# Two spectral-MLP layers: edge columns of z from small turns, and the turns of z at other places

## The chip, the cores and the metric

The kernel runs on one core of one Trainium2 chip. The metric is the time of one execution on the device in microseconds (us), lower is better. An execution that was profiled also has a span, from its first to its last instruction.

## The reference

The computation is one layer "A" and one layer "B", done twice, on 2048 rows (S) of 512 channels (D), with F = 1376. All data are float32.

```python
def _A_ref(x, dft_seq_re, dft_seq_im, dft_hid_re, dft_hid_im):
    a = jnp.einsum("bsd,ed->bse", x, dft_hid_re)
    b = jnp.einsum("bsd,ed->bse", x, dft_hid_im)
    y = jnp.einsum("ts,bse->bte", dft_seq_re, a) - jnp.einsum("ts,bse->bte", dft_seq_im, b)
    return y

def _B_ref(x, w1, w2, w3, w4):
    h = _gelu(_layernorm(x, axis=-1) @ w1)
    # four groups of 128 channels, shifted by +1, -1, +2, -2 rows (zeros at the ends)
    hs = jnp.concatenate([g0, g1, g2, g3], axis=-1) @ w2
    x1 = x + hs
    h2 = _gelu(_layernorm(x1, axis=-1) @ w3) @ w4
    return x1 + h2

x = A_x
x = x + _A_ref(_layernorm(x, axis=-1), ...)
x = x + _B_ref(_layernorm(x, axis=-1), ...)
# and both once more
```

## The kernel before

Every product is made of three matmuls of 128 x 512: a float32 operand is split into a high part (cast to fp32r) and a low part (the rest), and high x high, high x low and low x high are summed in PSUM (`mm3`, lines 261 to 263). ScalarE (ACT) makes the high parts, VectorE (DVE) the low parts. Instructions run on each engine in the order in which the program writes them; `hook` functions and the lists in `late` place side work between the steps of a loop. SyncE (SP) issues all transfers, in program order, and a transfer that must wait holds back the ones behind it.

A layer has these stages. The rows are cut into four chunks (c = 0 to 3) of 512.

- **x stage and y stage** of chunk c (`x_phase`, `y_phase`) multiply by the sequence matrix. Pieces of that matrix of 512 KB come through four raw buffers (`raw`, lines 190, 208 to 224) and are split into four ring buffers. A y stage is 192 matmuls. The product of chunk c with the hidden matrix (`hid`) is made inside the x stage of chunk c + 1; that of chunk 3 stands by itself after its y stage, as four steps of 24 matmuls. The operands `rr` of those steps are finished just before by DVE and ACT work called `re1`, `im1+`, `re0+` and so on (`run_late`).
- **z of a chunk** is its layer-normed rows, turned so that the channels lie on the partitions. A turn is made in parts: ACT normalizes a tile of 128 rows (line 309), DVE turns it in 32 x 32 blocks (`turn_one`, line 555), SP stores the four strips to DRAM (`turn_out`, line 563) and loads them back in the other order (`turn_in`, line 568), and `zt_split` (lines 573, 574) makes high and low parts, in two pieces of 128 x 1024. `zt[0]` and `zt[1]` hold two chunks in turn, each with two edge columns on either side (HALO) that belong to the neighbour chunks.
- **`shifted(c)`** multiplies z of chunk c by w1: four groups of 12 matmuls each, for channels shifted by -1, -2, +1 and +2 columns in that order. The first two groups read the left edge, the last two the right edge. Each group ends in a gelu (line 607) and a split (608, 609).
- **`mixed(c)`** multiplies by w2 (four blocks of 12 matmuls), adds the normed x and gives `x1s`. Those are normed and turned in the same way into `rt` (`rt_split`).
- **`mlp(c)`**: 13 steps t, most of 24 matmuls, on `rt`. `shifted`, `mixed` and the turns of the chunk after are called between its steps.

Before, z of chunk 0 is loaded from `x1d` in the x stage of chunk 3, normed and turned there, and loaded back in that chunk's y stage (k = 4). Chunk 1 is normed in the y stage, turned after the third `hid` step and loaded behind the weights w1. Chunk 2 is normed and turned in `shifted(0)` and loaded in `mixed(0)`; chunk 3 is turned in `mlp(0)`. The right edge of chunk c is copied from the loaded chunk c + 1:

```python
def right_halo(c):
    v = ztf[(c + 1) % 2][:, :, 1, HALO : 2 * HALO]
    hi, lo = (zt[c % 2][:, :, i, HALO + CH :] for i in range(2))
    nc.scalar.copy(hi, v)                                                  # line 594
    nc.vector.tensor_tensor(lo, v, hi.bitcast(F32), op=ALU.subtract)       # line 595
```

Of the kernel before, what the change touches and what calls it, by code (L numbers as in the profile page):

```python
# [13 lines left out]
P = 128  # L14
# [6 lines left out]
NC = S // CH  # L21
# [4 lines left out]
B = 32  # L26
# [9 lines left out]

FIRST, X6, X7 = (1, 3, 5, 8, 11, 13), 2, 4
HAT = (2, 3, 3, 4, 5, 5, 6, 6)
BACK = {1: (4,), 2: (6,), 4: (8,), 5: (10,)}
HORDER = ((1, 0), (0, 1), (1, 1), (0, 0))  # L40


# [1 line left out]
def spectral_mlp_kernel(ctx: ExitStack, tc: tile.TileContext, x, ws, hs, w1, w2, w34, out):  # L44
# [263 lines left out]
    def normed_act(o, s, mr):  # L308
        nc.scalar.activation(o, s, AF.Identity, bias=mr[2], scale=mr[1])  # L309
# [237 lines left out]
    def blocks_of(u):  # L547
        return u.rearrange("p (d a i) -> p d a i", d=KD, a=NB)

    def blocks_in(t, q):  # L550
        return t.rearrange("p d (a q j) -> p d a q j", a=NB, q=TC)[:, :, :, q]

    def turn_one(t, q, u=None):
        v = blocks_in(t, q)
        nc.vector.transpose(v, v if u is None else blocks_of(u))
# [9 lines left out]
    def turn_in(dst, col):  # L565

        z = zd[count["turn"] % 2].rearrange("(d p) t -> p d t", p=P)
        nc.sync.dma_start(dst[:, :, 1, col : col + CH], z)
# [18 lines left out]
        if c == NC - 1:  # L587
            nc.vector.memset(zt[c % 2][:, :, :, HALO + CH :].bitcast(F32), 0.0)

    def right_halo(c):  # L590

        v = ztf[(c + 1) % 2][:, :, 1, HALO : 2 * HALO]
        hi, lo = (zt[c % 2][:, :, i, HALO + CH :] for i in range(2))
        nc.scalar.copy(hi, v)
        nc.vector.tensor_tensor(lo, v, hi.bitcast(F32), op=ALU.subtract)
# [81 lines left out]
    pairs = [tmp[:, 2 * i : 2 * i + 2] for i in range(3)]  # L677
    X1 = pairs[2]
    Z = tmp[:, 0:4]
    singles = [tmp[:, 4], tmp[:, 5], spare[:, 0], spare[:, 1]] + [tmp[:, i] for i in range(4)]  # L680
    warm = const.tile([P, 1], F32, name="warm")
    nc.scalar.activation(warm, mhalf[:, 0, 0:1], AF.Gelu_apprx_tanh)

    for layer in range(LAYERS):
# [4 lines left out]
        for c in range(NC):  # L689
# [74 lines left out]
            def hook(i):  # L764
                k, odd = divmod(i, 2)
                if layer == 0 and c == 1:
                    if i == 1:
                        xp_sums(NP - 1)
                    if i == 2:
                        xp_highs(NP - 1, False)  # L770
                    if i == 3:
                        xp_lows(NP - 1, False)
                if c == 0:
                    if layer:
                        for k, first in ((6, X6), (7, X7)):
                            for step, f in zip((0, 1, 3, 4, 6), xp_stages):
                                if i == first + step:
                                    f(k)
                    return
                j = (c - 1) * TC  # L780
                if i == 4:
                    rows(X1, xin, j, 2, True)
                if i == 9:
                    rows(X1, x1d, j, 2, False)
                if i == 10:
                    rows(X1, xin, j + 2, 2, True)
                if c == NC - 1:
                    if i == 6:
                        for q in range(TC):
                            nc.sync.dma_start(blocks_in(Z, q), blocks_of(x1d[q * P : (q + 1) * P, :]))  # L790
                    if 0 <= i - 9 < 4:
                        u = blocks_in(Z, i - 9)
                        normed_act(u, u, ln2[i - 9])
                    if 0 <= i - 11 < 4:
                        turn_one(Z, i - 11)
                    if i == 15:
                        turn_out(Z)

            x_phase(c, hook)

            def hook(k):
                if k == 1 and c:
                    rows(X1, x1d, (c - 1) * TC + 2, 2, False)
                if c == NC - 1:
                    for j in BACK.get(k, ()):
                        rows(xs[j // 2], x1d if j < 12 else xin, j, 2, True)
                    if k == 4:
                        turn_in(ztf[0], HALO)
                    if k in (4, 5):
                        for j in (2 * k - 4, 2 * k - 3):  # L810
                            normed_act(blocks_in(Z, j - TC), blocks_of(xt(j)), ln2[j])

            y_phase(c, hook)

# [4 lines left out]
        for i, (ri, dp) in enumerate(HORDER):  # L819
            if i == 1:  # L820
                run_late("im1")
            if i == 3:
                state["limit"] += 2
            s = stream()
            hid(ri, dp, s, acc4, 0, i == 0, i == 3)
            j = (0, 2, 12, 14)[i]
            rows(xs[j // 2], x1d if j < 12 else xin, j, 2, True)
            if i == 0:
                run_late("re1", "im1+")
            if i == 1:  # L830
                run_late("re0+", "re0++")
            if i == 2:
                run_late("re0")
                for q in range(TC):
                    turn_one(Z, q)
                turn_out(Z)
                zt_split(0)
                edges(0)
                zs.update(norm_z(range(8, 10)))
        w1p = [stream(), stream()]  # L840
        turn_in(ztf[1], HALO)
        zs.update(norm_z(range(10, 12)))
        state["limit"] += 2
        w2p = [stream(), stream()]

        def hook(n):
            if n == 0:
                right_halo(0)
            turn_one(turn2, n, zs.pop(8 + n))
            if n == 3:  # L850
                turn_out(turn2)

        shifted(0, w1p, hook)
        mrs = []

        def hook(q, x1s):
            if q == 0:
                turn_in(ztf[0], HALO)
                zt_split(1)
                left_halo(2)  # L860
            if q % 2:
                mrs.extend(stats(x1s[q - 1 : q + 1]))
# [3 lines left out]
        def hook(n):  # L866
            if n == 0:
                finish_z3(0, x1s, mrs)
                for q in range(TC):
                    turn_one(turn2, q, x1s[q])  # L870
                turn_out(turn2)
                right_halo(1)
# [18 lines left out]
        for c in range(NC):  # L891
            for t in mlp(c):
                if t == 1 and c:
                    for j in range((c - 1) * TC, c * TC, 2):
                        rows(xs[j // 2], dst, j, 2, False)
                if c == 0:
                    if t == 0:
                        add_y(NC - 1, 1, PB, xs[7], "14")
                    if t in (3, 4):
                        run_late(str(6 + 2 * t))  # L900
                    if t in (5, 6):
                        zs.update(norm_z((2 + 2 * t, 3 + 2 * t)))
                    if t in (7, 8):
                        for q in (2 * t - 14, 2 * t - 13):
                            turn_one(turn_z, q, zs.pop(12 + q))
                    if t == 8:
                        turn_out(turn_z)
                    if t == 10:
                        turn_in(ztf[1], HALO)
                    if t == 11:  # L910
                        zt_split(0)
                        left_halo(NC - 1)
                    if t == 12:
                        zt_split(1)
                        edges(NC - 1)
                        right_halo_of(2)
                if c + 1 < NC:
                    if c > 0 and t == 0:
                        shifted(c + 1, w1p)
                    if c > 0 and t == 1:  # L920
                        x1s = mixed(c + 1, w2p)
                    n = t - 1 if c else t
                    if n == 1:
                        mrs = stats(x1s)
                    if n in (2, 3):
                        finish_z3(c + 1, x1s, mrs, (2 * n - 4, 2 * n - 3))
                    if n in (3, 4):
                        turn_z3(c + 1, x1s, (2 * n - 6, 2 * n - 5))
                    if n == 4:
                        turn_out(turn_r[(c + 1) % 2])  # L930
                    if n == 6:
                        turn_in(rtf[(c + 1) % 2], 0)
# [65 lines left out]
```

## Time and profile before

| | before |
|---|---|
| time, median of 3 runs | 1508.55 us (1508.46 to 1509.02) |
| the profiled execution | 1509.24 us, of which 1507.5 us are its span |
| mean granted TensorE clock | 0.992 |
| busy: PE, DVE, ACT, POOL | 98%, 74%, 45%, 6% of the span |
| moved by DMA | 246.5 MB, 164 GB/s over the span |

PE is TensorE, POOL is GpSimd, SPq is SyncE's queue of transfers. A profile row of a matmul shows its start, its length, and, in brackets, how long PE was idle before it and what ended that wait. Matmuls overlap: in a dense stream one starts every 0.227 us though each is shown with 0.39 us. The two layers run the same stages; the stage of chunk 3 that the change touches lies at about 303 to 476 us in the first layer and at about 1045 to 1220 us in the second.

### The profile page before, as it was taken

How to read it: one execution, taken by the hardware profiler on the slowest of the kernel's cores; microseconds unless marked ns; L12 is line 12 of the kernel's file. 1: busy time of each engine (PE TensorE's matmuls, PEld its weight loads, DVE VectorE, ACT ScalarE, POOL GpSimd, SP SyncE). 2: the span in 40 equal slices, each digit the busy share in tenths (PEclk: the TensorE clock that was granted, in tenths of full speed). 3: DMA queues.
4: the chain of work that ended last, by engine and by line, in shares of the span. 5: the costliest groups of instructions: out<-in, count | busy, mean ns of one | idle time of the engine just before them, and what ended most of it. 6: DMA issues, size and time to landing. Idle time of an engine off the chain costs nothing.

```text
span 1507.5 us, 17227 instructions
## 1 busy us (share of the span) xinstructions
PE 1471.5 (98%) x6408; PEld 1207.6 (80%) x6408; DVE 1123.0 (74%) x1548; ACT 684.8 (45%) x873; POOL 89.1 (6%) x101
## 2 busy tenths in 40 slices
PE   9999999999888999999999999999989799999998
PEld 7888888887777888887888888888867688888887
DVE  6876987979757756568899879899878576654553
ACT  5564454554444443335544544445535254332331
POOL 2100000000001100001100000000000010000000
PEclk9999999999999999999999999999999899999999
DMA  7336656587553534333435565655776437243440
GB/s 238 125 100 199 211 171 225 169 238 259 201 168 116 161 129 126 103 114 107 137 127 187 190 218 173 208 202 163 230 261 210 126 123 208 83 128 98 126 147 35
DMA packets 127156, 246.50 MB, mean 164 GB/s; under 512 B 24544, under 2 KB 57312, under 8 KB 127072
## 3 DMA queue, kind: packets, MB, share of 16 engines
q1 hardware_dynamic: 127072, 245.40, 50.7%
q8 instruction: 50, 0.82, 0.2%
q14 instruction: 34, 0.28, 0.1%
HBM read 213.91 MB, written 31.46 MB: 163 GB/s over the span
## 4 chain that ended last, share of the span: by engine, by line
PE 82%; DVE 10%; DMA 4%; issue 2%; ACT 2%; SPq 0%; POOL 0%; DVEq 0%; ACTq 0%; POOLq 0%
PE psd L263 9%; PE psd L262 9%; PE psd L261 9%; PE psa L262 8%; PE psa L261 8%; PE psa L263 8%; PE psc L261 6%; PE psb L263 6%; PE psc L262 6%; PE psc L263 6%; PE psb L262 5%; PE psb L261 5%; DVE ring L224 3%; DMA raw<-in_ws 2%; DMA zt1f<-zd 1%
## 5 line engine op out<-in xcount | busy, mean ns | idle before, releaser
L208 ACT CAST ring<-raw 128x1024 fp32r<-128x1024 f32 (+1 forms) x231 | 226.7, 987 | 184.0 <-PE psb L263 110.4
L224 DVE TENSOR_TENSOR ring<-raw,ring 128x1024 fp32r<-128x1024 f32 (+1 forms) x231 | 262.9, 1143 | 27.1 <-ACT ring L208 27.1
L608 DVE CAST h<-tmp 128x512 fp32r<-128x512 f32 x70 | 29.8, 426 | 101.8 <-ACT tmp L607 101.8
L607 ACT ACTIVATE tmp<-psd 128x512 f32<-128x512 f32 x60 | 35.8, 596 | 132.7 <-PE psd L263 90.3
L261 PE MATMUL psd<-ring,rr 128*128 128x512 f32 x208 | 80.9, 389 | 0.0
L262 PE MATMUL psd<-ring,rr 128*128 128x512 f32 x208 | 80.9, 389 | 0.0
L263 PE MATMUL psd<-ring,rr 128*128 128x512 f32 x208 | 80.9, 389 | 0.0
L263 PE MATMUL psd<-rt,ring 128*128 128x512 f32 x176 | 68.6, 390 | 0.6 <-DVE ring L224 0.6
L263 PE MATMUL psa<-rt,ring 128*128 128x512 f32 x176 | 68.6, 390 | 0.0
L261 PE MATMUL psd<-rt,ring 128*128 128x512 f32 x176 | 68.5, 389 | 0.0
L262 PE MATMUL psd<-rt,ring 128*128 128x512 f32 x176 | 68.5, 389 | 0.0
L262 PE MATMUL psa<-rt,ring 128*128 128x512 f32 x176 | 68.5, 389 | 0.0
L261 PE MATMUL psa<-rt,ring 128*128 128x512 f32 x176 | 68.5, 389 | 0.0
L261 PE MATMUL psc<-ring,h 128*128 128x512 f32 x176 | 68.5, 389 | 0.0
L262 PE MATMUL psc<-ring,h 128*128 128x512 f32 x176 | 68.5, 389 | 0.0
L263 PE MATMUL psc<-ring,h 128*128 128x512 f32 x176 | 68.5, 389 | 0.0
L261 PE MATMUL psb<-ring,h 128*128 128x512 f32 x176 | 68.5, 389 | 0.0
L262 PE MATMUL psb<-ring,h 128*128 128x512 f32 x176 | 68.5, 389 | 0.0
L263 PE MATMUL psb<-ring,h 128*128 128x512 f32 x176 | 68.5, 389 | 0.0
L301 POOL TENSOR_TENSOR rs<-ve,mhalf 128x4 f32<-128x4 f32 x16 | 27.7, 1728 | 624.3 <-DVE nm L300 624.3
L280 POOL TENSOR_TENSOR rs<-ve,mhalf 128x2 f32<-128x2 f32 (+2 forms) x27 | 37.9, 1402 | 441.5 <-DVE nb L279 441.5
L309 ACT ACTIVATE tmp<-xs,nb,rs 128x512 f32<-128x512 f32 x66 | 50.5, 808 | 19.2 <-POOL nb L281 19.2
(297 smaller groups left out, 3977.6 us busy)
## 6 DMA issues: line engine op xcount, KB each, us to landing
raw<-in_ws SPq DMA_DIRECT2D x183, 512.0 KB, 4.9
raw<-in_w SPq DMA_DIRECT2D x80, 512.0 KB, 3.6
raw<-in_hs SPq DMA_DIRECT2D x56, 512.0 KB, 3.6
raw<-in_w SPq DMA_DIRECT2D x32, 256.0 KB, 3.0
x1d<-tmp SPq DMA_DIRECT2D x12, 512.0 KB, 6.9
xs<-x1d SPq DMA_DIRECT2D x12, 512.0 KB, 7.5
zd<-turnr SPq DMA_DIRECT2D x24, 256.0 KB, 4.0
xs<-in_x SPq DMA_DIRECT2D x9, 512.0 KB, 6.8
```

The source lines that it names most:

```text
L208: nc.scalar.copy(dest[:, a:b, 0], r[0][:, a:b])
L224: nc.vector.tensor_tensor(lo, src, hi.bitcast(F32), op=ALU.subtract)
L261: nc.tensor.matmul(o, lh, rh, start=first, stop=False)
L262: nc.tensor.matmul(o, lh, rl, start=False, stop=False)
L263: nc.tensor.matmul(o, ll, rh, start=False, stop=last)
L280: nc.gpsimd.tensor_tensor(rs[:, :n], ve[:, :n], mhalf[:, 0, :n], op=ALU.pow)
L301: nc.gpsimd.tensor_tensor(rs, ve, mhalf[:, :, :2], op=ALU.pow)
L309: nc.scalar.activation(o, s, AF.Identity, bias=mr[2], scale=mr[1])
L607: nc.scalar.activation(g_of, ps_of, AF.Gelu_apprx_tanh)
L608: nc.vector.tensor_copy(dst[:, 0], g)
```

## The change

`right_halo(c, u)` no longer reads the loaded neighbour chunk. It takes u, the first normed tile of chunk c + 1, turns its first 32 rows (B) with four TensorE transposes into a PSUM bank, and takes the two edge columns from there. The four trips of z through DRAM move to later places, and with them the loads of the rows that they start from:

- chunk 0: its rows are loaded in the y stage of chunk 3 (`BACK`), normed at its k = 4 and 5, turned after the first `hid` step, loaded after the third; `zt_split(0)` and the edges follow the splits of w1.
- chunk 1: normed around `hid` and in `shifted(0)`, turned and stored in its first two groups, loaded at its end, split in `mixed(0)`.
- chunks 2 and 3: normed, turned, loaded and split in `mlp(0)` (chunk 3's split at the start of `mlp(1)`); `shifted(2)` and `mixed(2)` are called two steps of `mlp(1)` later.

```diff
-BACK = {1: (4,), 2: (6,), 4: (8,), 5: (10,)}
+BACK = {1: (0,), 2: (2,), 4: (4,)}
...
-    def right_halo(c):
-
-        v = ztf[(c + 1) % 2][:, :, 1, HALO : 2 * HALO]
+    def right_halo(c, u):
+
+        ps = mm_bank()
+        for d in range(KD):
+            nc.tensor.transpose(ps[:, d * B : (d + 1) * B], u[:B, d * P : (d + 1) * P], ident[:B, :B])
+        v = ps[:, : KD * B].rearrange("p (d t) -> p d t", d=KD)[:, :, :HALO]
...
-    singles = [tmp[:, 4], tmp[:, 5], spare[:, 0], spare[:, 1]] + [tmp[:, i] for i in range(4)]
+    singles = [spare[:, 0], spare[:, 1], tmp[:, 4], tmp[:, 5]] + [tmp[:, i] for i in range(4)]
...  # x stage of chunk 3
-                if c == NC - 1:
-                    if i == 6:
-                        for q in range(TC):
-                            nc.sync.dma_start(blocks_in(Z, q), blocks_of(x1d[q * P : (q + 1) * P, :]))
-                    if 0 <= i - 9 < 4:
-                        u = blocks_in(Z, i - 9)
-                        normed_act(u, u, ln2[i - 9])
-                    if 0 <= i - 11 < 4:
-                        turn_one(Z, i - 11)
-                    if i == 15:
-                        turn_out(Z)
...  # y stage of chunk 3
-                    if k == 4:
-                        turn_in(ztf[0], HALO)
                     if k in (4, 5):
-                        for j in (2 * k - 4, 2 * k - 3):
-                            normed_act(blocks_in(Z, j - TC), blocks_of(xt(j)), ln2[j])
+                        for j in (2 * k - 8, 2 * k - 7):
+                            normed_act(blocks_in(Z, j), blocks_of(xt(j)), ln2[j])
...  # the four hid steps i
-            j = (0, 2, 12, 14)[i]
-            rows(xs[j // 2], x1d if j < 12 else xin, j, 2, True)
+            if i < 2:
+                j = (6, 8)[i]
+                rows(xs[j // 2], x1d, j, 2, True)
             if i == 0:
-                run_late("re1", "im1+")
-            if i == 1:
-                run_late("re0+", "re0++")
-            if i == 2:
-                run_late("re0")
+                run_late("re1")
                 for q in range(TC):
                     turn_one(Z, q)
                 turn_out(Z)
-                zt_split(0)
-                edges(0)
-                zs.update(norm_z(range(8, 10)))
+                run_late("im1+")
+            if i == 1:
+                run_late("re0+", "re0++")
+                zs.update(norm_z((4,)))
+            if i == 2:
+                run_late("re0")
+                turn_in(ztf[0], HALO)
+                zs.update(norm_z((5,)))
         w1p = [stream(), stream()]
-        turn_in(ztf[1], HALO)
-        zs.update(norm_z(range(10, 12)))
+        right_halo(0, zs[4])
+        zt_split(0)
+        edges(0)
...  # shifted(0), after group n
-            if n == 0:
-                right_halo(0)
-            turn_one(turn2, n, zs.pop(8 + n))
+            if n == 0:
+                zs.update(norm_z((6, 7)))
+            if n < 2:
+                for q in (2 * n, 2 * n + 1):
+                    turn_one(turn2, q, zs.pop(4 + q))
+            if n == 1:
+                turn_out(turn2)
+                rows(xs[5], x1d, 10, 2, True)
+                zs.update(norm_z((8,)))
+            if n == 2:
+                rows(xs[6], xin, 12, 2, True)
             if n == 3:
-                turn_out(turn2)
+                turn_in(ztf[1], HALO)
+                rows(xs[7], xin, 14, 2, True)
...  # mixed(0), after block q
             if q == 0:
-                turn_in(ztf[0], HALO)
+                right_halo(1, zs.pop(8))
+            if q == 2:
                 zt_split(1)
                 left_halo(2)
...  # mlp(0), step t: chunk 2 from t = 5, chunk 3 from t = 8
+                    for base, first, zf in ((8, 5, ztf[0]), (12, 8, ztf[1])):
+                        n = t - first
...
-                    n = t - 1 if c else t
+                    n = t - (0, 3, 1)[c]
```

Three places of the instruction order, the same in both layers. First DVE, from the end of the y stage of chunk 3 to the start of `shifted(0)`; line 387 makes the low part of an `rr`, 426 the sums before it, 555 the turns, 598 is the line of the low edge that stood at 595.

```order
 L387 TENSOR_TENSOR rr_144<-rr01f,rr_144 128x2x512 [waits Activation_49]
+L555 STREAM_TRANSPOSE tmp<-tmp 128x16x32 x4
 L426 TENSOR_TENSOR rr11f<-rr11f,tmp 128x2x512
 L387 TENSOR_TENSOR rr_146<-rr11f,rr_146 128x2x512 [waits Activation_49]
-L224 TENSOR_TENSOR ring_166<-raw,ring_166 128x2x512 [waits DMAHW6_49,PE_49]
+L224 TENSOR_TENSOR ring_166<-raw,ring_166 128x2x512 [waits DMAHW4_49,PE_49]
 L426 TENSOR_TENSOR rr00f<-rr00f,beside 128x2x512
 L426 TENSOR_TENSOR rr00f<-rr00f,beside 128x2x512 [waits DVE_49]
 L387 TENSOR_TENSOR rr_140<-rr00f,rr_140 128x2x512 [waits Activation_49]
-L555 STREAM_TRANSPOSE tmp<-tmp 128x16x32 x4
```

The four turns moved from behind the last low part of the `rr` (of chunk 1's rows) to a place ahead of the sum for the third `hid` step (of chunk 0's rows).

Second DVE as it is now, at the start of `shifted(0)` and in `mixed(0)`. A name DMAHW with a number is the counter of one transfer: DMAHW7 here is that of `zt0f<-zd`, DMAHW2 that of `zt1f<-zd`. Line 574 is `zt_split`, 585 the zeros of the first left edge, 641 the sum in `mixed`.

```order
L598 TENSOR_TENSOR zt_115<-psd_174,zt_115 128x4x2 [waits DMAHW7_49,Activation_49]
L574 TENSOR_TENSOR zt_115<-zt0f,zt_115 128x2x512 [waits Activation_49] x2
L585 MEMSET zt_115 128x8x2 [waits DVE_49]
...
L641 TENSOR_TENSOR spare<-psd_175,spare 128x512 [waits PE_49,Activation_49]
L598 TENSOR_TENSOR zt_117<-psa_168,zt_117 128x4x2 [waits DMAHW2_49,Activation_49]
L641 TENSOR_TENSOR tmp<-psa_169,tmp 128x512 [waits PE_49,Activation_49]
```

The edge columns are now written from PSUM, and their instruction waits for the load of the chunk into the same tile; the split of that chunk and the zeros stand behind it.

Third SP, from chunk 3's y stage to `shifted(0)`: 181 are row loads, 190 raw pieces, 563 the stores and 568 the load of a trip.

```order
+L190 DMA raw<-in_w 128x1024 x3
+L181 DMA xs_127<-x1d 128x2x512
 L563 DMA zd_81<-tmp 32x16x128 x4
-L190 DMA raw<-in_ws 128x1024 x2
-L181 DMA x1d<-tmp 128x2x512
-L181 DMA xs_126<-x1d 128x2x512
-L190 DMA raw<-in_ws 128x1024 x2
-L181 DMA xs_127<-x1d 128x2x512
-L190 DMA raw<-in_ws 128x1024 x4
+L190 DMA raw<-in_w 128x1024
 L181 DMA xs_128<-x1d 128x2x512
 L568 DMA zt0f<-zd_81 128x4x512
```

Chunk 0's trip stood among the pieces of the sequence matrix (`in_ws`), and now stands among the weights (`in_w`), with one weight and one row load between its stores and its load.

More of the change, by code (lines that the diff above doesn't have):

```diff
@@ L871, in hook @@
                 turn_out(turn2)
-                right_halo(1)
             if n == 2:
@@ L900, in spectral_mlp_kernel @@
                         run_late(str(6 + 2 * t))
[L901 to L909, printed above, removed]
+                    for base, first, zf in ((8, 5, ztf[0]), (12, 8, ztf[1])):
+                        n = t - first
+                        if n in (0, 1):
+                            zs.update(norm_z((base + 2 * n, base + 2 * n + 1)))
+                        if n in (1, 2):
+                            for q in (2 * n - 2, 2 * n - 1):
+                                turn_one(turn_z, q, zs.pop(base + q))
+                        if n == 2:
+                            turn_out(turn_z)
+                        if n == 4:
+                            turn_in(zf, HALO)
                     if t == 11:
                         zt_split(0)
[L912 to L916, printed above, removed]
+                if c == 1 and t == 0:
+                    zt_split(1)
+                    left_halo(NC - 1)
+                    edges(NC - 1)
+                    right_halo_of(2)
                 if c + 1 < NC:
-                    if c > 0 and t == 0:
+                    n = t - (0, 3, 1)[c]
+                    if c > 0 and n == -1:
                         shifted(c + 1, w1p)
-                    if c > 0 and t == 1:
+                    if c > 0 and n == 0:
                         x1s = mixed(c + 1, w2p)
-                    n = t - 1 if c else t
                     if n == 1:
```

## The prediction

> **What bounds the kernel now.** The first page shows a kernel that lives on PE.
>
> ```profile
> PE 1471.5 (98%) x6408; PEld 1207.6 (80%) x6408; DVE 1123.0 (74%) x1548; ACT 684.8 (45%) x873; POOL 89.1 (6%) x101
> ```
>
> So only PE's idle time, 36 us of the span, and matmuls at a slow clock can be won. The view of waits says whom PE waits for (line, releaser, total, times, longest).
>
> ```profile
> PE psa L261 <- ACT zt L594: 15.9, 4, 4.0
> PE psc L262 <- DVE ring L224: 6.5, 3, 3.1
> PE psb L262 <- DVE ring L224: 3.0, 4, 1.0
> ```
>
> Line 594 is the right edge: four waits of 4 us, two in each layer. The ring waits are late pieces of the sequence matrix. Next I cut the trace by stages: the y stage of chunk 2, which nothing touches; the y stages of chunk 3 in both layers; and from the first `hid` matmul to the first of `mlp(0)` in both layers.
>
> ```profile
> 215.95:259.50 43.55, 43.55 (x193) 36.06 (x193) 34.21 (x41) 19.35 (x24) 2.83 (x2) 1.00 0.63 212
> 346.57:395.53 48.96, 44.75 (x193) 35.92 (x193) 40.19 (x43) 24.81 (x30) 2.23 (x2) 1.00 0.77 267
> 1088.81:1139.95 51.14, 46.05 (x193) 36.88 (x193) 41.63 (x44) 26.11 (x33) 1.38 (x2) 0.97 0.75 258
> 395.53:476.39 80.86, 71.06 (x290) 56.60 (x288) 55.81 (x80) 35.20 (x49) 3.48 (x6) 0.94 0.56 176
> 1139.95:1220.07 80.12, 71.69 (x290) 56.99 (x289) 54.38 (x79) 33.88 (x46) 3.78 (x6) 0.94 0.56 176
> ```
>
> A y stage of 192 matmuls takes 43.55 us undisturbed, 0.2268 us each. Chunk 3's lose 5.4 and 7.6 us. The transition has 288 matmuls, 65.3 us; it loses 15.6 and 14.8 us. Of the 15.6, 1.5 is a `hid` wait (row below), so the edges and the clock take 14.1, and 14.6 in the second layer after 0.2 of the same.
>
> The clock is the third item: matmul rows after waits.
>
> ```profile
> 384.75 0.50 PE L262 MATMUL psc<-ring,ay 128*128 128x512 f32 x1 [3.13 <-DVE ring L224]
> 397.51 0.50 PE L263 MATMUL psc<-ring,rr 128*128 128x512 f32 x1 [1.37 <-DVE rr L387]
> 429.26 0.80 PE L261 MATMUL psa<-zt,w 128*128 128x512 f32 x1 [3.99 <-ACT zt L594]
> 434.13 0.51 PE L263 MATMUL psa<-zt,w 128*128 128x512 f32 x1
> 1127.85 0.79 PE L262 MATMUL psc<-ring,ay 128*128 128x512 f32 x1 [3.05 <-DVE ring L224]
> ```
>
> After the wait of 3.99 us the 12 matmuls of one group need 4.87 us from first to last start, against 11 x 0.2268 = 2.5: the drop costs 2.4 more. A wait of 3.05 brought it (0.79 instead of 0.50), one of 3.13 did not.
>
> **The change, part by part.** *The y stage.* The late piece has this row on DVE, and these on SP and in the chain.
>
> ```profile
> 382.33 1.23 DVE L214 TENSOR_TENSOR ring1f<-raw 128x1024 f32<-128x1024 f32 x1 [4.49 <-DMA raw<-in_ws]
> 346.88 3.94 SPq L563 DMA_DIRECT2D zd<-tmp  x4
> 370.12 0.46 SPq L568 DMA_DIRECT2D zt0f<-zd  x1
> 373.33 1.46 SPq L190 DMA_DIRECT2D raw<-in_ws  x2
> 373.77 8.44 DMA raw<-in_ws
> ```
>
> The piece took 8.44 us because the 1 MB load of z stood 3 us ahead of it. Both that load and the stores at 346.88 leave the stage, with four turns and one row load; three row loads stay, at the old places. With chunk 2's stage as the pattern (no loss) and DVE still busy 40.2 of 43.55 us, I leave a loss of 0.5: won are 4.9 and 7.1, together 12.0 us. Bounds: 0 if DVE or the row loads keep the pieces late, 13 if nothing is left. What is late next is the `hid` wait of 1.4 us: it may go (-1.5) or appear in the second layer too (+1.5); I take it as it is. The x stage loses no PE wait, so its 4 norms, 4 turns and 8 transfers are free there.
>
> *The steps of `hid`.* Rows of DVE:
>
> ```profile
> 401.04 1.23 DVE L387 TENSOR_TENSOR rr<-rr01f,rr 128x1024 fp32r<-128x1024 f32 x1
> 410.40 1.23 DVE L387 TENSOR_TENSOR rr<-rr00f,rr 128x1024 fp32r<-128x1024 f32 x1 [1.12 <-ACT rr L384]
> 411.54 2.48 DVE L555 STREAM_TRANSPOSE tmp<-tmp 128x512 f32<-128x512 f32 x4
> ```
>
> The four turns now stand behind the row at 401.04, so the low part at 410.40 ends at 414.1 instead of 411.6. PE, dense from 397.51, reaches its third matmul of the fourth step at 397.51 + 72 x 0.2268 = 413.8: 0.2 us lost, where before there were 2 us of room. `hid` ends at 419.0 (before 418.8).
>
> *Three trips in a row.* Now z of chunk 0, z of chunk 1 and `rt` each take a trip through DRAM that starts only in this transition. What trips cost:
>
> ```profile
> 439.91 3.63 SPq L563 DMA_DIRECT2D zd<-turn  x4
> 446.84 0.38 SPq L568 DMA_DIRECT2D zt0f<-zd  x1
> 458.61 3.09 SPq L563 DMA_DIRECT2D zd<-turn  x4
> 465.19 0.38 SPq L568 DMA_DIRECT2D rt0f<-zd  x1
> 421.57 7.37 DMA zt1f<-zd
> DMA to landing us min/median/max: 5.6/7.1/9.2
> 415.17 1.06 ACT L573 CAST zt<-zt0f 128x1024 fp32r<-128x1024 f32 x1 [3.85 <-DVE zt L574]
> 416.25 1.23 DVE L574 TENSOR_TENSOR zt<-zt0f,zt 128x1024 fp32r<-128x1024 f32 x1 [1.12 <-ACT zt L573]
> 429.01 0.20 ACT L594 CAST zt<-zt1f 128x8 fp32r<-128x8 f32 x1 [5.69 <-DMA zt1f<-zd]
> 474.55 1.22 DVE L574 TENSOR_TENSOR rt<-rt0f,rt 128x1024 fp32r<-128x1024 f32 x1
> ```
>
> From the stores to the load's issue: 6.6 to 6.9 us. From issue to landing: 5.6 to 9.2 (the loads of line 568). A split piece is a high part and then a low part, 2.3 us; the second high part waits for the first low one, so a split takes 4.7.
>
> Wait A, before `shifted(0)` (first layer's clock). The turns end at 404.7, the load is issued at 411.4, and lands at 418.4: I take 7.0, since a weight and a row load go just ahead of it, as at 421.57 (7.37). The order shows that the edge columns wait for this load, then come the split and the zeros of the left edge, which the first matmul reads: 0.4 + 4.7 + 0.1, so PE starts at 423.6 and has waited since 419.0: A = 4.6, longer than the wait of 3.99 after which the clock dropped: +2.4 for the slow group. The four small turns run in this wait. Their nearest row is the warm-up:
>
> ```profile
> 1.36 4.33 PE L114 MATMUL psd<-ident 128*128 128x128 f32 x24 [1.36 <-POOL mhalf L57]
> ```
>
> These are 12 matmuls, in two rows each: 0.36 us for one at four times the width, so four take under 1.5 us; those in `mixed(0)` stand on PE's path, I take 0.5 (0 to 1.5). The Trainium skill, page "TensorE: Matmul & The Clock Gate", section "PE-mode transpose", says that such turns do not count as activity for the clock gate; no run here shows it, and the drop after A is in my sum already.
>
> Wait B, before `shifted(1)`. With the slow first group PE ends the second group at 431.5. Rows of the work from there:
>
> ```profile
> 457.83 0.58 ACT L607 ACTIVATE tmp<-psd 128x512 f32<-128x512 f32 x1
> 435.76 0.69 DVE L609 TENSOR_TENSOR rg<-tmp,rg 128x512 fp32r<-128x512 f32 x1
> 436.37 0.70 DVE L555 STREAM_TRANSPOSE turn<-spare 128x512 f32<-128x512 f32 x1
> 437.97 0.81 ACT L309 ACTIVATE tmp<-xs,nb,rs 128x512 f32<-128x512 f32 x1
> 444.41 0.68 DVE L638 TENSOR_TENSOR tmp<-psd,tmp 128x512 f32<-128x512 f32 x1
> 446.61 0.16 DVE L279 TENSOR_SCALAR nb<-mv 128x2 f32<-128x2 f32 x1
> 452.94 1.29 DVE L648 TENSOR_TENSOR xs<-xs,tmp 128x512 f32<-128x512 f32 x2
> ```
>
> Gelu 0.6, split 1.1, two turns 1.3: the stores start at 434.5, the load is issued 6.6 later at 441.1, and lands after 6.5 (two row loads just ahead) at 447.6. PE, free of waits, is done with `shifted(0)` and `mixed(0)` at 431.5 + 6 x 2.72 + 0.5 = 448.3. But `right_halo(1)` stands after the first block of `mixed(0)`, and both its copies wait for that landing; behind them wait ACT's norms and DVE's sums of the other blocks, and behind those the split. From the landing: edge 0.3, two norms 1.6, high part 1.1, done at 450.6. On DVE a sum and its statistics (444.41 to 446.77, 2.4), another sum 0.6 and the low part 1.2 after the first norm: 452.9; second piece 455.2. The first group's eighth matmul needs that; it ends at 456.5 instead of 451.0: B = 5.5. It is broken into waits of about 2.3, 2.3 and 0.9, all below 3.05, so I add no drop (bounds 0 and 2.4).
>
> Wait C, before `mlp(0)`. From 455.2: last sum and statistics 2.4, gelu split 1.1, then from 452.94 to 458.61 it was 5.7 with a POOL wait of about 1.3 in it, now 5.0: stores at 463.8. From stores to the end of the `rt` split it was 458.61 to 475.77, 17.2: ready at 481.0. PE gets there at 456.5 + 8.2 + 10.9 = 475.6 and ends its first group at 482.2 instead of 478.3: C = 3.9.
>
> Sum for the transition: 0.2 + 4.6 + 2.4 + 0.5 + 5.5 + 3.9 = 17.1 us, against 14.1 and 14.6 before: +3.0 and +2.5. In `mlp(0)` and `mlp(1)`, where chunks 2 and 3 go and DVE has room, I count 0: every trip there has at least three steps of 5.4 us.
>
> Total: -12.0 + 5.5 = -6.5. The profiled execution took 1509.24 us (the span and 1.7 around it), 0.69 above the median of 1508.55. 1509.24 - 6.5 - 0.7 = 1502.0 us.
>
> The Trainium skill (same page, section "HAM oscillation") says that the clock falls after an idle gap of about 3.4 us. Here 3.05 sufficed once. By its number A, 4.6 us long, drops the clock as in my sum; less up to 1.5 of turns inside it, it might just not, and each layer would be 2.4 us shorter (a part of the first rival).
>
> **The rivals.** *Quick trips*: loads land in 5.6 us, as the shortest did, and the clock holds after A. A becomes 3.2, B 4.6: 12.4 per transition, -3.9 over both, with -12.0 and the `hid` wait gone (-1.5): 1491 us. For it: the transition moves only 176 GB/s. Against: a row or weight load goes ahead of two of the trips. Chance 0.20.
>
> *Slow trips, slower than before*: the place is the three loads of line 568 in the transition, now in a chain. If they land in 9.2 us, as the slowest did, A, B and C grow by 2.2, 2.7 and 3.6, 8.5 per layer: -6.5 + 17 = +10.5, 1519 us. It decides from 1.1 us more per trip than I took (6.5 over six trips). For it: the median is 7.1, and loads go ahead of two of the trips. Against: the stages of the longest ones moved 267 GB/s, this one 176. Chance 0.15.
>
> *The y stage stays half late*: DVE's 40.2 busy of 43.55 leaves no room for its own waits on ACT, and half of the 12 us stays: 1508 us. Chance 0.13.
>
> *The change doesn't do what it says*: edges from small turns should be free of the neighbour's load, but the order makes each wait for a load into its own tile. That is part of my sum; were it not to bind, B would be 2.5 and the total 6 us lower, inside the range.
>
> **How the numbers follow.** My forecast has 0.52, its own range 1497 to 1507 (C, B and the landings each by 1 us). Over 0.2% (3.0 us, about what a measurement of this kernel can tell) faster: 0.49 + 0.20 + 0.01 = 0.70; within it 0.03 + 0.08 + 0.03 = 0.14; slower 0.04 + 0.12 = 0.16. The range for 8 in 10 runs from the quick trips, 1490, to halfway into the slow ones, 1512.
>
> **What would show it.** Right: no PE wait for ring pieces over 1 us in chunk 3's y stages, each near 44 us; a wait of 4 to 5 us ahead of `shifted(0)` with matmuls of 0.6 us behind it; waits at `shifted(1)` and `mlp(0)` that end on the splits; transitions of 82 to 84 us. Wrong: y stages near 49 us, or transitions under 78 or over 88.

## The result, and the profile after

The changed kernel takes 1510.11 us (median of 12 runs, 1507.99 to 1512.72) against 1508.57 (1507.26 to 1510.44): a ratio of 1.001, interval 1.0001 to 1.0019. The forecast was 1502.0. The profiled execution took 1507.99 us, its span 1506.2; it is the fastest of the 12, about 2 us below the usual one. The same kernel run again gave 1508.96, ratio 1.0003 (0.9994 to 1.0012), with a span of 1507.2 in its profile. The first interval leaves out 1 by a hair and the second holds it, so there is no gain, and a loss of 0.2% at most.

First the stages of the changed kernel. The view of windows (start and end, length, busy time of PE, PEld, DVE, ACT, POOL with their counts, granted clock, DMA share, GB/s) for chunk 3's y stages in both layers:

```profile
346.80:390.32 43.52, 43.52 (x193) 36.05 (x192) 39.60 (x43) 24.61 (x30) 2.23 (x2) 1.00 0.67 235
1088.28:1131.80 43.52, 43.52 (x194) 36.05 (x192) 39.48 (x42) 24.20 (x29) 1.38 (x2) 1.00 0.66 236
```

They were 48.96 and 51.14 us; both are now 43.52, with PE busy all the time. 13.1 us are won.

The transition is best cut a little later than in the prediction, from the first `hid` matmul to 48 matmuls into `mlp(0)`, so that all of wait C lies inside: 336 matmuls, which at 0.2268 us take 76.2. First the kernel before, then the changed one:

```profile
395.53:487.27 91.74, 81.94 (x338) 65.61 (x336) 64.56 (x100) 38.87 (x54) 3.99 (x7) 0.94 0.49 155
1139.95:1230.95 91.00, 82.57 (x338) 66.00 (x337) 63.13 (x99) 37.54 (x51) 4.29 (x7) 0.94 0.49 155
```

```profile
390.32:486.74 96.42, 82.88 (x346) 65.33 (x344) 63.46 (x100) 39.04 (x53) 5.13 (x7) 0.95 0.49 153
1131.80:1229.69 97.89, 84.49 (x345) 66.66 (x344) 63.85 (x100) 39.44 (x54) 4.48 (x7) 0.93 0.49 151
```

It loses 15.5 and 14.8 us before, 20.2 and 21.7 after (22.1 and 21.1 in the second profile of the changed kernel): 4.7 and 6.9 us more. -13.1 + 11.6 is -1.5, and the spans differ by 1.3. The gain of the y stages is there in full; the transition has eaten it.

PE's waits in the changed kernel (line, releaser, total, times, longest) name the places:

```profile
PE psa L261 <- ACT w L208: 5.3, 1, 5.3
PE psd L261 <- ACT w L208: 5.3, 1, 5.3
PE psa L261 <- ACT zt L573: 3.5, 1, 3.5
PE psd L261 <- ACT zt L573: 2.9, 1, 2.9
PE psd L262 <- DVE zt L574: 2.0, 1, 2.0
PE psc L263 <- DVE rr L387: 1.7, 2, 1.1
PE psa L262 <- DVE zt L574: 1.7, 1, 1.7
PE psa L262 <- DVE rt L574: 1.4, 2, 0.8
PE psd L262 <- DVE rt L574: 1.4, 2, 0.8
```

The four 4 us waits for line 594 are gone. In their place stand A (5.3, once a layer, ahead of `shifted(0)`), B (3.5 and 1.7, 2.9 and 2.0, ahead of and inside `shifted(1)`) and C (the `rt` rows, and two more of 0.9 and 0.7 for the high part of `rt`). The `rr` row is a short wait inside `hid` in each layer. The name in A's rows misleads: `w` was rounded, but the last thing to end was the zeros of the left edge. Rows from the timeline of the first layer, PE and the engines it waits for:

```profile
413.33 0.43 PE L594 MATMUL psd<-ident,spare 32*128 32x32 f32 x4
413.80 0.17 ACT L597 CAST zt<-psd 128x8 fp32r<-128x8 f32 x1 [3.68 <-PE psd L594]
414.00 0.17 DVE L598 TENSOR_TENSOR zt<-psd,zt 128x8 fp32r<-128x8 f32 x1 [2.44 <-ACT zt L597]
414.19 1.05 ACT L573 CAST zt<-zt0f 128x1024 fp32r<-128x1024 f32 x1 [0.23 <-DVE zt L598]
415.27 1.23 DVE L574 TENSOR_TENSOR zt<-zt0f,zt 128x1024 fp32r<-128x1024 f32 x1 [1.11 <-ACT zt L573]
417.61 1.23 DVE L574 TENSOR_TENSOR zt<-zt0f,zt 128x1024 fp32r<-128x1024 f32 x1 [1.11 <-ACT zt L573]
418.91 0.07 DVE L585 MEMSET zt<- 128x16 f32 x1
419.08 0.76 PE L261 MATMUL psd<-zt,w 128*128 128x512 f32 x1 [5.32 <-ACT w L208]
419.65 0.63 PE L262 MATMUL psd<-zt,w 128*128 128x512 f32 x1
```

It is a circle that leaves PE and comes back to it: the four small turns wait on PE for the end of `hid`; behind them the edge, behind the edge the split, behind the split the zeros, behind the zeros PE. At the end the clock has dropped (0.63 a matmul). B is the same shape in `mixed(0)`, with a load in it:

```profile
429.28 3.11 SPq L563 DMA_DIRECT2D zd<-turn  x4
432.43 1.44 SPq L181 DMA_DIRECT2D xs<-x1d  x1
433.91 1.07 SPq L181 DMA_DIRECT2D xs<-in_x  x1
435.92 0.36 SPq L568 DMA_DIRECT2D zt1f<-zd  x1
444.22 0.17 ACT L597 CAST zt<-psa 128x8 fp32r<-128x8 f32 x1 [11.14 <-DMA zt1f<-zd]
444.28 1.52 ACT L309 ACTIVATE tmp<-xs,nb,rs 128x512 f32<-128x512 f32 x2
445.70 1.04 ACT L573 CAST zt<-zt1f 128x1024 fp32r<-128x1024 f32 x1
446.79 0.80 PE L261 MATMUL psa<-zt,w 128*128 128x512 f32 x1 [3.53 <-ACT zt L573]
449.28 0.79 PE L262 MATMUL psa<-zt,w 128*128 128x512 f32 x1 [1.69 <-DVE zt L574]
449.87 0.63 PE L263 MATMUL psa<-zt,w 128*128 128x512 f32 x1
```

The load lands 8.3 us after its issue, behind two row loads; the edge is released by it, and two norms stand on ACT between edge and split.

### The profile page after: what moved, and what is told of

It is laid out like the page before. It is cut to its first block, busy times and chain, and to the rows that moved or that the text cites. A ratio compares the mean times of both kernels' runs of the same rounds, so it can differ in the third digit from the quotient of the medians.

```text
span 1506.2 us, 17251 instructions
## 1 busy us (share of the span) xinstructions
PE 1471.2 (98%) x6424; PEld 1208.3 (80%) x6424; DVE 1121.9 (74%) x1548; ACT 685.4 (46%) x875; POOL 92.7 (6%) x101
## 4 chain that ended last, share of the span: by engine, by line
PE 84%; DVE 7%; DMA 5%; ACT 2%; issue 1%; SPq 1%; POOL 0%; DVEq 0%; ACTq 0%
PE psd L262 9%; PE psd L263 8%; PE psd L261 8%; PE psa L262 7%; PE psa L263 7%; PE psa L261 7%; PE psc L263 6%; PE psc L261 6%; PE psb L263 6%; PE psc L262 6%; PE psb L261 6%; PE psb L262 6%; DVE ring L224 2%; DMA zd<-turn 1%; DMA zt1f<-zd 1%; DMA raw<-in_ws 1%
## 5 line engine op out<-in xcount | busy, mean ns | idle before, releaser
L224 DVE TENSOR_TENSOR ring<-raw,ring 128x1024 fp32r<-128x1024 f32 (+1 forms) x231 | 262.8, 1142 | 27.0 <-ACT ring L208 26.6
L309 ACT ACTIVATE tmp<-xs,nb,rs 128x512 f32<-128x512 f32 x82 | 62.6, 807 | 21.6 <-POOL nb L281 19.2
L610 ACT ACTIVATE tmp<-psd 128x512 f32<-128x512 f32 x46 | 27.5, 597 | 88.3 <-PE psd L263 59.8
L610 ACT ACTIVATE tmp<-psa 128x512 f32<-128x512 f32 x45 | 26.8, 597 | 86.2 <-PE psa L263 54.2
```

The costliest lines, as they stand in the source:

```text
L224: nc.vector.tensor_tensor(lo, src, hi.bitcast(F32), op=ALU.subtract)
L610: nc.scalar.activation(g_of, ps_of, AF.Gelu_apprx_tanh)
```

## The experiments

Below, the loss of a transition is the length of the window above less 76.2 us; "slow clock" behind a wait is what the matmuls behind it that last over 0.52 us take beyond 0.2268 from start to start (idle time not counted). The ratio is always to the kernel before, run on the same chip.

### The two circles, one at a time

Run `split_first` breaks A's circle at the edge:

```
+        zt_split(0)
+        edges(0)
         right_halo(0, zs[4])
-        zt_split(0)
-        edges(0)
```

> Only the order of three lines changes: zt_split(0) and edges(0) now stand ahead of right_halo(0), not behind it. Theory (the circle): the four small turns stand on PE behind the last hid step, the edge copies wait for them, the split waits behind the copies on ACT and DVE, and PE waits for the split; so the wait ahead of shifted(0) is at least 5.3 us whatever the load does. With the split first it starts when the load has landed, about 412 us, and ends 4.7 us later, at 417 instead of 419: the wait falls from 5.3 to about 3.3 us in each layer, 4 us less in all, 1506 us. Rival (my prediction's step): the split waits for the landing of z of chunk 0, the order does not matter, and the time stays within 1 us of 1510.

Measured: 1504.87 us, ratio 0.9974 (0.9964 to 0.9985). From the small turns to the first shifted matmul 4.6 and 4.4 us instead of 5.75. The timeline shows the landing that the edge had hidden:

```profile
413.22 1.05 ACT L573 CAST zt<-zt0f 128x1024 fp32r<-128x1024 f32 x1 [2.95 <-DMA zt0f<-zd]
417.94 0.07 DVE L585 MEMSET zt<- 128x16 f32 x1
418.11 0.76 PE L261 MATMUL psd<-zt,w 128*128 128x512 f32 x1 [4.19 <-issue]
```

The load had landed at 413.2, before PE's turns were even done; the turns and the edge cost the split 1 us. So the circle was there, but worth less than I expected (the wait fell to 4.2 and 4.0, not to 3.3). Most of A is what is left: two halves of the split and the zeros. The time fell by more than the wait; in the one profile the rest is spread over B and slow rows.

Run `edge_late` takes chunk 1's edge out of the way of its split, run `loads_behind` the row loads out of the way of its load:

```
-            if q == 0:
-                right_halo(1, zs.pop(8))
             if q == 2:
                 zt_split(1)
                 left_halo(2)
+                right_halo(1, zs.pop(8))
```

> Only right_halo(1) moves: from behind the first block of mixed(0) to behind zt_split(1), after the third. Theory (queues held): the edge copy waits for the load of z of chunk 1 (11.1 us on ACT, 9.1 on DVE), and two norms, two sums and statistics wait behind it, which then delay the split by 2.8 us after the landing at 444.2. With the edge behind the split, the low part of the first piece starts about 2.5 us sooner, the second wait ahead of shifted(1) (1.7 and 2.0 us) is gone or below 0.5, and the total falls by 2 to 3 us in each layer: 1504.5 to 1506. Rival (load bound): the split starts at the landing as before, nothing but the first wait counts, and less than 1 us is won.

```
-                rows(xs[5], x1d, 10, 2, True)
...
-                rows(xs[6], xin, 12, 2, True)
             if n == 3:
                 turn_in(ztf[1], HALO)
+                rows(xs[6], xin, 12, 2, True)
                 rows(xs[7], xin, 14, 2, True)
+                rows(xs[5], x1d, 10, 2, True)
```

> Only the row loads of chunks 2 and 3 (xs 5 and 6, 512 KB each) move: from between the stores and the load of chunk 1's trip to behind that load. Theory (crowded trip): the load landed 8.3 us after its issue at 435.9; free of the 1 MB ahead it takes about 6.0, so the wait ahead of shifted(1) falls by 2.3 us in each layer, 4.6 in all, 1505.5 us. Rival: the row loads are drained by then and the landing is as long by itself; no change within 0.7 us.

Measured: 1504.12 (0.9968, 0.9956 to 0.9981) and 1503.72 (0.9966, 0.9952 to 0.9979). Without the edge in front, the split follows the landing at once and PE waits 1.6 and 0.8:

```profile
444.17 1.05 ACT L573 CAST zt<-zt1f 128x1024 fp32r<-128x1024 f32 x1 [9.30 <-DMA zt1f<-zd]
446.52 0.60 PE L262 MATMUL psa<-zt,w 128*128 128x512 f32 x1 [0.76 <-DVE zt L574]
```

With the row loads behind, the load takes 5.7 us instead of 8.3 (issue on SP, then the edge that it releases; in this profile the layer runs 3.1 us later by then, so the clock times are not to be compared with those above):

```profile
439.01 0.38 SPq L568 DMA_DIRECT2D zt1f<-zd  x1
444.71 0.17 ACT L597 CAST zt<-psa 128x8 fp32r<-128x8 f32 x1 [8.49 <-DMA zt1f<-zd]
```

So B had two causes of about the same weight, the queue ahead of the load and the order behind it. The unaltered kernel ran beside these three:

> The changed kernel once more, unaltered, for a second profile and a second set of times. Its profiled execution took 1507.99 us, the fastest of 12 (1507.99 to 1512.72, median 1510.11), so that profile shows 2 us less than a usual run. Theory (the clock): the spread comes from how long the slow clock lasts after the waits ahead of shifted(0) and shifted(1), four of them in an execution, 1.4 to 2.8 us each. Then a profile near the median has the same waits within 0.3 us and about ten more matmul rows of 0.63 us. Rival (the loads): it comes from landings of the three trips, and a slower profile has longer waits with the same number of slow rows.

Its 1508.96 and the waits (A 5.3 twice, B 3.1 + 2.0 and 3.9 + 1.7) repeat within 1 us, and the slow rows move from layer to layer: behind A and B there are 42 instead of 37. The second layer's B is 0.7 us longer, so neither theory alone gives the spread.

### The three edits in one

> The three edits of the runs before (the split of chunk 0 ahead of its edge, the edge of chunk 1 behind its split, two row loads behind the load of chunk 1) in one kernel. Alone they measured 4.1, 4.8 and 5.2 us less than the changed kernel's 1509. Theory that the lost time is two separate circles on PE (ahead of the first and of the second group of shifted matmuls): the first edit adds to either of the other two, but those two work on the same wait B (4.9 us with its pieces before, about 2.4 left with the one, 3.1 with the other; the split chain alone keeps some), so the sum is less than 14: about 9 to 11, time 1499. Rival, that each edit only shifts the phase of the transition and the loss turns up at the next place (wait C ahead of the mlp, whose turns start later when PE arrives earlier): no better than the best of the three alone, 1504.

Measured: 1496.71 us, ratio 0.992 (0.9907 to 0.9934). The transitions lose 15.6 and 16.2 us, 5.4 less each than in the changed kernel (mean of its four). That is 12 us below the 1508.96 of the unaltered kernel, more than the 9 to 11 that I expected and a little less than the 14 of the three alone: A and B are two places, and their cures nearly add.

### Chunk 0's trip at its old place

Run `old_place_0` undoes one part of the change alone:

```
+                    if i == 6:
+                        for q in range(TC):
+                            nc.sync.dma_start(blocks_in(Z, q), ...)
...
+                    if k == 4:
+                        turn_in(ztf[0], HALO)
...
-                turn_in(ztf[0], HALO)
+                zt_split(0)
+                edges(0)
```

> Undoes one part alone: chunk 0's z is again loaded, normed, turned and stored in the x stage of chunk 3, read back in its y stage, and split behind the third step of hid; chunk 1's later trip and the small turns stay. Theory: the y stages lose what they lost before (about 5 and 7 us: 48.5 and 50.5 us instead of 43.5), and wait A (5.3 us with 1.7 of slow clock, twice) shrinks to the edge alone, the four turns and two small copies, about 1.3 us: 12 back, 11 to 12 won, time 1508 to 1511, no change: the move of chunk 0 pays for its gain one for one. Rival 1, that the gain of the y stages came from the lighter row loads or from chunk 1's turn: y stages stay near 43.5 and the time falls to 1498. Rival 2, that wait A is not the edge's circle but the weights that ACT rounds there: wait A stays, 1520.

Measured: 1504.87, ratio 0.9977 (0.9966 to 0.9987): 4 to 5 us better than the changed kernel, where I expected no change. Two rows of y stages and two of transitions:

```profile
347.08:397.47 50.39, 46.27 (x193) 37.06 (x193) 41.64 (x44) 23.49 (x28) 2.23 (x2) 0.97 0.74 251
1086.41:1135.06 48.65, 44.63 (x192) 35.92 (x193) 40.01 (x43) 21.87 (x25) 2.17 (x2) 1.00 0.74 257
397.47:484.69 87.22, 80.56 (x345) 64.19 (x344) 60.26 (x95) 38.30 (x52) 3.92 (x7) 0.98 0.45 144
1135.06:1224.58 89.52, 81.78 (x345) 64.78 (x344) 61.90 (x96) 39.67 (x55) 3.48 (x7) 0.96 0.45 141
```

The y stages lose their 12.0 us again, as expected: it was chunk 0's trip that slowed them. But the transitions lose only 11.0 and 13.3, against a mean of 21.3 in the changed kernel: moving chunk 0 costs 9 us a layer there, not the 6 that I had counted for A. From the turns to the first shifted matmul it is 0.36 us, and no slow row follows. So the change has two parts of opposite sign: all of it but chunk 0's trip (the small turns, chunk 1's later trip, the other moves) gains about 3.5 us (1508.29 to 1504.87), and chunk 0's later trip gives back 4 to 5.

Run `old_place_mended` is this with the two cures of B.

> Chunk 0's trip at its old place (the run old_place_0, 1504.9) with chunk 1's edge behind its split and the two row loads behind its load. Theory that wait B is a circle of its own: 4.5 and 4.3 us of waits and the slow rows behind them shrink to about 1 us as in the kernel with the three edits (there 6 to 7 us in the two layers against the one without): 1497 to 1499. This then says what chunk 0's later trip is worth once both circles are mended: the three edits reached 1496.7, so nearly nothing, because its 12 us in the y stages are paid with wait A. Rival, that B's cure needs PE's later arrival that wait A brings: 1502 to 1504.

Measured: 1496.4 (0.9919, 0.9905 to 0.9934), level with the 1496.71 of the three edits at the new place. B shrinks without PE's later arrival, to two waits of 0.3 and 0.7 in each layer, so it stands by itself. And chunk 0's later trip is worth nothing so long as the rest of A stands: about 102 us of y stages and 168 of transitions here, 87 and 184 there.

### The clock behind wait A

Runs `busy_in_a` (on the changed kernel, 12 matmuls) and `all_busy` (on the three edits, 10) let PE work while it waits:

```
+        for _ in range(12):
+            nc.tensor.matmul(mm4[count["mm"] % 4][:, :P], ident, ident, start=True, stop=True)
         shifted(0, w1p, hook)
```

> Adds 12 matmuls of the identity (as those that warm the clock at the start, about 0.4 us each) behind the small turns of chunk 0, into the bank that the first shifted group then starts afresh; nothing waits for them. Wait A of 5.3 us stays as long, but PE works in it. Theory that the slow rows behind A (9 matmuls at 0.42 instead of 0.227 us, 1.7 us) come from PE's idleness: they go, in both layers, 3.4 us less, 1505.5. Rival, that they come from something else at that place (the split's or the weights' traffic, an aligned window of the clock): the slow rows stay and the time is 1509, or up to 1510 if the added matmuls end later than the split.

> The three edits together with 10 identity matmuls in what is left of wait A (4.2 us). Theory as for the single runs: what the three reach together, less 1.7 in each layer for the slow clock behind A: about 1496. Rival, that the clock falls anyway (behind wait B or C) or the added matmuls end too late: the same as the three together.

Measured: 1507.17 (0.999, 0.9981 to 0.9999) and 1494.09 (0.9906, 0.9891 to 0.9921). In `busy_in_a` the 12 took 2.9 us and not the 4.8 I had counted, so an idle 2.45 was left in both layers. First layer, then the second:

```profile
419.64 0.77 PE L261 MATMUL psd<-zt,w 128*128 128x512 f32 x1 [2.45 <-ACT w L208]
...
1156.12 2.94 PE L856 MATMUL psa<-ident 128*128 128x128 f32 x24
1161.52 0.47 PE L261 MATMUL psa<-zt,w 128*128 128x512 f32 x1 [2.46 <-ACT w L208]
```

The same rest of a wait brought the slow clock in one layer and not in the other. In `all_busy` only 0.8 and 1.4 are left, and no slow row follows in either layer: `shifted(0)` to `mixed(0)` takes 11.21 us twice, against 12.72 and 13.42 with the three edits alone. So the slow rows behind A come from PE's idleness, at 1.5 to 2.2 us a time, as far as one profile of each kernel shows. The medians differ by 2.6, the two profiled spans by 3.9 (1496.2 and 1492.3); the two ratios' intervals overlap, so the times alone do not show the gain. Wait C became longer in the second layer (3.5 instead of 2.1).

### What in wait A has to be waited for

Run `memset_first` adds one line's move to the three edits: the zeros of the left edge go ahead of the split.

```
+        nc.vector.memset(zt[0][:, :, :, :HALO].bitcast(F32), 0.0)
         zt_split(0)
-        edges(0)
+        left_halo(1)
```

> The three edits together, and besides the left edge's zeros are written ahead of chunk 0's split instead of behind it on DVE. The kernel with the three edits: 1496.7, wait A 4.0 and 4.1 us, ending as the zeros are written. Theory that PE's first shifted group needs the zeros and the first half of the split (the first low part ends 2.4 us earlier), not the small edge: the wait falls to about 1.8 us with one of about 0.7 behind it, 1.5 less a layer, and up to 1.7 more if the clock stays: 1490.5 to 1494. Rival, that PE waits for the whole of the split's tile: no change, 1496.7.

Measured: 1492.02, ratio 0.9893 (0.9878 to 0.9907), the lowest median of all, though not to be told from the next run's. PE's rows in the first layer:

```profile
413.37 0.43 PE L594 MATMUL psd<-ident,spare 32*128 32x32 f32 x4
414.16 0.50 PE L261 MATMUL psd<-zt,w 128*128 128x512 f32 x1 [0.37 <-ACT zt L573]
415.42 0.49 PE L262 MATMUL psd<-zt,w 128*128 128x512 f32 x1 [0.76 <-DVE zt L574]
417.76 0.51 PE L262 MATMUL psd<-zt,w 128*128 128x512 f32 x1 [0.68 <-DVE zt L574]
```

Of the 4.4 us from turns to matmuls 0.8 is left, with two waits of 0.7 behind it, and the clock holds there (in the first layer it falls later, behind B's waits of 1.50 and 0.76). A 0.07 us instruction at the end of a queue had made PE wait for the whole split, where PE needs the split only a piece at a time.

Run `turn_earlier` (also on the three edits) starts chunk 0's trip in the y stage instead:

```
+                    if k in (5, 6):
+                        for q in (2 * k - 10, 2 * k - 9):
+                            turn_one(Z, q)
+                    if k == 7:
+                        turn_out(Z)
```

> The three edits together, and chunk 0's four turns move from behind the first hid step into the y stage (two each behind its sixth and seventh pairs), its stores to the last pair, its load behind the first hid step, its split behind the third. Theory that A is the trip's end meeting PE, and that 7 us more of lead take it away: no wait ahead of the first shifted group but for the turns, no slow rows, 5.9 us less a layer; the turns cost the y stage at most 1 us each as DVE has 3 us free: 1485 to 1488. Rival, that DVE's 2.5 us or the stores on SP ahead of the weight loads make the sequence's pieces late or the hid steps wait: y stage 45 to 47 us, or waits in hid of 2 us and more, 1490 to 1494.

Measured: 1492.53 (0.9895, 0.9878 to 0.9911): 5 us too little, and where the rival put it. A is gone (0.35 us from turns to matmuls), but `hid` takes 26.6 us in both layers instead of 23.5, and the y stages 0.4 and 1.2 us longer: the turns on DVE push back what `hid` waits for, and even these short waits bring slow rows.

```profile
392.14 0.49 PE L262 MATMUL psc<-ring,rr 128*128 128x512 f32 x1 [0.79 <-DVE ring L224]
394.41 0.50 PE L263 MATMUL psc<-ring,rr 128*128 128x512 f32 x1 [1.78 <-DVE rr L387]
395.71 0.63 PE L262 MATMUL psb<-ring,rr 128*128 128x512 f32 x1
```

## Why the prediction was wrong

*The y stage* was right: 12.0 us forecast, 13.1 measured, with PE busy for all of its 43.52 us; `old_place_0` shows that it is chunk 0's trip that had cost them.

*The transition* was wrong: +3.0 and +2.5 us forecast, +4.7 and +6.9 measured, +6.6 and +6.3 in the second profile. Means over those four transitions, term by term:

| term | forecast | measured |
|---|---|---|
| A, with its turns | 4.6 | 5.75 |
| slow clock behind A | 2.4 | 2.0 |
| turns in `mixed(0)` | 0.5 | 0.36 |
| B | 5.5 | 5.2 |
| slow clock behind B | 0 | 2.1 |
| C | 3.9 | 2.1 |
| sum of these | 16.9 | 17.5 |
| the rest, without waits of `hid` | 0.2 | 2.7 |

The failed step is the line "17.1 us, against 14.1 and 14.6 before". The 14.1 was a difference: length of the stage less ideal matmuls. It held two waits of 4.0, 4.1 us of slow clock (4.6 in the second layer), and some 2.1 of small losses that I had not named (a `shifted` of 48 matmuls without any wait, for one, takes 11.21 us and not 10.89). The 17.1 was a sum of named terms, without them. Compared like with like, the forecast would have been 2.1 us a layer dearer, 4.2 in all: 1506 instead of 1502. That is the larger part of the miss of 7 to 8 us, and no rival of mine held it. Of the rest, the named terms came out 0.6 us a layer dearer, and the unnamed losses grew from 2.1 to 2.7.

The trace says what these losses are. From the starts of the matmuls on either side, a wait at full clock costs 0.2 to 0.3 us more than the idle time that the view shows: row 1188.98 below starts 2.50 us before the next, of which 1.99 is shown as idle, and a dense matmul takes 0.23. The transition had five waits before and has eight now, which makes some 1.0 us of such losses into 1.8; the dense rows lose another 0.6 to 0.9.

The prediction's own sign was too weak to show this. Cut at the first matmul of `mlp(0)`, as there, the transitions take 83.4 and 84.8 us, against 82 to 84 called right; some 2 us of the added loss of each layer come in the 48 matmuls behind that cut, where wait C lies.

The terms themselves were off by more than their sum. That B, cut into pieces "all below 3.05", brings no drop was false: it dropped each time, in the second layer after 2.88, one matmul at 0.50 and 1.99 (rows below). C was smaller than I took by about as much; B's slow clock lies ahead of it and gives the `rt` trip time, though no run took the two apart. In A I had the order of edge, split and zeros, but took the load's landing for what releases them, where PE's own small turns do, so I did not see the circle: the load landed at 413.2, as forecast (418.4 less the 5.2 by which this stage now starts earlier), but PE's own turns ended only at 413.8. Chunk 1's load took 8.3 us, not 6.5, behind its two row loads.

*`mlp`* was right at 0: from the end of the transition's window to the next y stage of chunk 3 it is 601.54 us before and after, and from the second window to the end 276.55 and 276.51.

The rival *Slow trips* has one of its three loads right: chunk 1's was 1.8 us slower than I took, and `loads_behind` won 5 us with that load alone; chunk 0's came when forecast. The rival *The y stage stays half late* is refuted. "The change doesn't do what it says" is closest in mechanism: an edge that is made to be free of the neighbour's load stood in the queue ahead of its own chunk's split, and moving it back won 4 to 5 us at each of the two places.

Open is why chunk 0's move costs 9 us a layer where A's gap and its slow clock show 7.4 (5.75 and 2.0, less 0.36 of turns): the rest lies in `hid`, B and slow rows, which shift by 1 to 2 us from one execution to the next.

## What to carry to other kernels

A transfer moved out of one stage was paid here where its result is next needed; move it only together with the order behind it, since what stands in the queue between landing and first use (an edge, a norm, 0.07 us of zeros) becomes part of the wait. Where the first piece of a split tile is enough to start, nothing that the start needs may stand behind the last piece. And compare a sum of named losses only with a sum of named losses: here the difference against the ideal held 2 to 3 us a layer without a name, and more of them with each further wait.

## What the runs showed of the hardware

The slow clock does not follow from the length of one wait. In the second layer of the changed kernel it came after two shorter ones with a matmul at 0.50 between them:

```profile
1188.98 0.50 PE L261 MATMUL psd<-zt,w 128*128 128x512 f32 x1 [2.88 <-ACT zt L573]
1191.48 0.80 PE L262 MATMUL psd<-zt,w 128*128 128x512 f32 x1 [1.99 <-DVE zt L574]
1192.07 0.63 PE L263 MATMUL psd<-zt,w 128*128 128x512 f32 x1
```

It came after 2.45 in one layer of `busy_in_a` and not after 2.46 in the other, a few matmuls after waits of 0.79 and 1.78 in `turn_earlier`, and not after 3.13 in the kernel before. The Trainium skill, page "TensorE: Matmul & The Clock Gate", section "What's actually happening", says that the clock gate watches PE's activity in a window of about 3.4 us that runs freely. That the same wait drops the clock at one time and not at another agrees with a window that is not tied to the wait; that a drop came after waits of 0.79 and 1.78 us does not fit a rule that wants a whole window idle. In the runs here a drop costs 1.3 to 3.0 us each time.
